# Pooled attention and token/channel mixing on one core: new positions for all attention steps, from a planner that knows later key loads and waits between half banks

## The chip, the cores and the metric

One core of one Trainium2 chip runs the whole program once. The time is device microseconds of one execution, taken as the median of several executions; lower is better. The engines are PE (matmul), ACT, DVE and POOL (elementwise work), and SP, which here only issues DMAs. PE writes its products to PSUM, which ACT and DVE read; POOL works on SBUF alone.

## The reference

```python
# q, k, v: (8, 8, 1152, 64); w_theta, w_ch: (512, 512); w_tok_r, w_tok_i: (576, 576)
q_pool = q.reshape(B, H, S // 2, 2, D).mean(axis=3)
scores = (1 / sqrt(D)) * q_pool @ k.transpose(0, 1, 3, 2)
attn = exp(scores - max(scores)); attn = attn / (sum(attn) + 1e-09)
x = (attn @ v), heads side by side                 # (8, 576, 512)
theta = x @ w_theta
zr, zi = x * cos(theta), x * sin(theta)
u = x + einsum('ts,bsd->btd', w_tok_r, zr) + einsum('ts,bsd->btd', w_tok_i, zi)
out = u + maximum(u @ w_ch, 0)
```

## The kernel before

There are two stages. The first, the attention, goes through 32 pairs of heads; the second goes through 8 batches of x. Weights arrive as 64-bit words and are turned to fp32 in 18 jobs that run beside the attention. The order of the second stage is written out and not touched here.

For a pair of heads the first stage does the following (names of steps as in the planner, lines as in the profile). SP loads q (`load_q`, L609), keys (`load_k`, L635) and v (`load_v`, L668). DVE adds neighbouring q rows (`pool_q`, L652); POOL takes two differences of key blocks (`diff0`, `diff1`, L659), which need all keys of the pair. DVE transposes the keys and q into PSUM (`t1`, L686; `t0`, L684), ACT copies this rounded (`hi10`, `hi0`, L713) and DVE makes the rest (`lo10`, `lo0`, L717). Key loads of the next pair wait for both transposes. PE makes products for the row maxima (`pm`, 15 steps, L730), DVE reduces them (`mx`, 15 steps, L742, then `nm` and `nt`, L750 and L753), and SP lays the negated maxima out (`load_max`, six DMAs, L765). PE makes the scores (`e`, 18 steps, L780), ACT exponentiates each (`x`, L790) into one of 14 buffers, POOL sums them up (`ss`, L797), and PE multiplies them with v (`av`, 18 steps, L802) and sums over keys (`ns`, L823). An exponential's buffer is free again when both `av` and `ss` (or `ns`) have read it. ACT copies the products out (`xu`, L814; `sm`, L834); SP and DVE divide by the sums through DRAM (`norm_...`, L839 to L883) and store x. A step such as x16 is the one of half u = 1 and key tile 6; ss01 and e18 likewise. Some three pairs are in flight at once.

PSUM in this stage is four tiles of two banks. `t`, `pm` and `e` take a tile; an `av` chain and the `ns` chain take one half (`acq=2`).

A weight job fetches (`w_fetch`, L934), splits words on ACT (`w_low`, `w_abs`, L944 and L948) and DVE (L952 to L969), puts them together on POOL (`w_mul`, `w_add`, L974 and L986); weights of the token mixing are then transposed on PE (`w_turn`, L1018 and L1023), the others are split again (L1000, L1005). After the last job its memory is given to x, and `early` issues the first load of x for the second stage (`xload`, L532).

All this is issued in an order that `schedule` finds when the program is built. Each step has an engine, an assumed duration and latency, and what it depends on; the planner runs a clock for the engines, PSUM and the buffers, and emits one step after the other. A step's position is `PLACE[step] + 18 * pair`, a weight step's `w0 + wd * job + wk * offset`. Between the first two pairs and the last, PE, ACT, DVE and POOL take their attention steps strictly in order of position (`ahead` is 1); SP looks 24 steps ahead, and the others 8 at the two ends. The next weight step of an engine is looked at as well, and goes first if its position is lower, or if by the planner's clock it is done before the other step could begin, give or take `slack`:

```python
if best is None or (at < far and (best[0] >= far or at + busy <= best[0] + PLACE["slack"])):
    best = (min(at, far), op, slot, busy)
```

On the chip each engine works its own list in order and waits at semaphores.

Of the kernel before, what the change touches and what calls it, by code (L numbers as in the profile page):

```python
# [25 lines left out]
    "load_k00": -34.88242, "load_k10": -32.47173, "load_k20": -41.45336, "load_k30": -28.50736,  # L26
    "diff00": -39.87507, "diff10": -35.75839, "load_q00": -64.34477, "load_q10": -75.25567,
    "load_q20": -35.82454, "load_q30": -61.16811, "pool_q00": -30.6917, "t10": -29.76226,
    "hi10": -18.79817, "lo10": -28.28938, "t00": -27.58235, "hi00": -17.63187, "lo00": -26.75167,
    "pm40": -19.09444, "mx40": -26.55706, "pm30": -18.78858, "mx30": -25.01085, "pm41": -17.19725,  # L30
    "mx41": -24.62429, "pm31": -17.04758, "mx31": -24.49251, "pm42": -16.56876, "mx42": -22.74469,
    "pm32": -16.06269, "mx32": -20.32787, "pm10": -12.92619, "mx10": -19.29508, "pm00": -15.38721,
    "mx00": -19.72983, "pm11": -11.3469, "mx11": -17.70748, "pm01": -10.92526, "mx01": -17.26176,
    "pm12": -9.29323, "mx12": -17.25916, "pm02": -9.11, "mx02": -16.98715, "pm20": -8.01255,
    "mx20": -16.13332, "pm21": -7.07965, "mx21": -15.98746, "pm22": -6.48707, "mx22": -13.57219,
    "nm00": -12.29583, "nt00": -11.25146, "load_max00": -9.16448, "load_max10": -19.75675,
    "load_max20": -9.6046, "load_max30": -38.55642, "load_max40": -12.38135,
    "load_max50": -76.95718, "e00": 0.83663, "x00": 2.47359, "e02": 1.73308, "x02": 4.44865,
    "e01": 1.85317, "e04": 2.06445, "x01": 5.17463, "x04": 6.56139, "ss01": -1.85432,
    "e03": 3.91959, "x03": 6.7328, "load_v00": -10.05597, "ss02": 1.71669, "e05": 7.91203,  # L40
    "ss03": 2.55261, "x05": 7.83833, "e06": 8.42872, "x06": 8.10801, "e10": 8.86747,
    "e07": 9.67362, "ss04": 3.13891, "x10": 9.26813, "x07": 9.74981, "e11": 10.10462,
    "e08": 10.39007, "x11": 10.98997, "ss05": 5.11849, "x08": 11.4556, "e13": 10.49512,
    "e12": 10.97372, "x13": 12.18436, "ss06": 12.66707, "x12": 14.01721, "e14": 11.21729,
    "e15": 11.32578, "x14": 14.22593, "av00": 12.28953, "x15": 14.10769, "e16": 13.47618,
    "e17": 12.6626, "av01": 12.39451, "ss11": 5.07143, "x16": 16.09668, "av02": 13.93027,
    "x17": 14.34836, "av10": 13.65905, "av03": 13.95031, "ss12": 5.61435, "av11": 13.86236,
    "av04": 14.10402, "av12": 13.94758, "ss13": 7.02357, "av05": 14.82141, "av13": 13.9736,
    "av06": 15.1885, "av14": 14.47683, "ss14": 10.7647, "av07": 18.30814, "av15": 14.8295,
    "av08": 18.38773, "ss15": 12.20219, "av16": 15.17117, "xu00": 20.33264, "e18": 17.01919,  # L50
    "ss16": 12.79139, "x18": 20.2032, "av17": 15.46904, "av18": 19.01658, "xu10": 21.82954,
    "ns00": 23.21575, "ns10": 23.58014, "ns20": 23.98061, "sm00": 25.00175,
    "norm_spread00": 3.09315, "norm_load00": 26.0753, "norm_recip00": 25.31238,
    "norm_save00": 35.09001, "norm_bcast00": 34.4841, "norm_bcast10": -37.21955,
    "norm_out00": 35.37772, "norm_store00": 63.75033, "norm_turn00": 39.55758,
    "norm_store10": -2.85209, "pool_q10": -44.60046, "ns30": -19.16538, "ns40": -12.30378,
# [1344 lines left out]
```

## Time and profile before

| | us |
|---|---|
| median of 3 executions | 1296.65 (1294.09 to 1301.59) |
| profiled execution | 1299.62 |
| its span | 1297.9 |
| attention, to the last run of av products with its end | 0 to about 834 |
| second stage | about 834 to 1297.9 |
| busy in the span: PE, DVE, POOL, ACT | 1229.5, 958.6, 804.6, 665.2 |

The profile is that of one execution. Ends of matmuls are modelled, since they overlap, so a busy PE is not a PE at its peak. "Waits" counts the idle time of an engine in front of an instruction by what ended it.

### The profile page before, as it was taken

What the parts mean: (1) busy time and instruction counts of PE and PEld (TensorE: products, weight loads), DVE (VectorE), ACT (ScalarE), POOL (GpSimd) and SP (SyncE); (2) the same over time, 40 slices, a digit from 0 to 9 for tenths busy, and PEclk for the clock granted to TensorE, in tenths of its full rate; (3) what the DMA queues carried; (4) which work ended last, traced back from release to release, by engine and by line L of the source; (5) the groups of instructions that cost most, each with busy time, mean ns of one, the idle gap of its engine ahead of it and who ended that gap; (6) DMA issues with size and microseconds to landing.
All of it is one profiled execution on the core that took longest, in us unless ns stands there. A gap on an engine that the chain in (4) does not pass through costs nothing.

```text
span 1297.9 us, 27681 instructions
## 1 busy us (share of the span) xinstructions
PE 1229.5 (95%) x10929; PEld 957.3 (74%) x10929; DVE 958.6 (74%) x1311; ACT 665.2 (51%) x1098; POOL 804.6 (62%) x600
## 2 busy tenths in 40 slices
PE   4899999999999998999999999789999999999998
PEld 2566667666666666666666766478999999999997
DVE  6889899989898988899999887265464645637452
ACT  1456556556656655666655665454443443444430
POOL 1678978988987987888889888324423233232320
PEclk9999999999999999999999999989999999999999
DMA  7445564555555447555546642404524425244221
GB/s 119 90 92 126 117 133 118 116 115 146 125 106 138 112 100 157 110 116 122 129 112 140 144 98 89 123 29 103 105 39 93 83 44 107 35 92 90 42 45 37
DMA packets 481201, 130.93 MB, mean 101 GB/s; under 512 B 450976, under 2 KB 451104, under 8 KB 481072
## 3 DMA queue, kind: packets, MB, share of 16 engines
q1 hardware_dynamic: 480896, 128.71, 46.9%
q8 instruction: 86, 1.41, 0.5%
q0 software_dynamic: 176, 0.46, 0.2%
q14 instruction: 43, 0.35, 0.1%
HBM read 97.21 MB, written 30.70 MB: 99 GB/s over the span
## 4 chain that ended last, share of the span: by engine, by line
PE 60%; DVE 10%; POOL 7%; SPq 7%; DMA 6%; ACT 6%; issue 4%; DVEq 0%; POOLq 0%; ACTq 0%
PE py L1221 16%; PE b L802 12%; PE b L780 11%; PE pr L1260 8%; PE pth L1133 7%; PE b L730 5%; POOL ss L797 5%; DVE mx L742 4%; SPq L635 3%; ACT pc L790 2%; PE b L823 2%; DMA dn<-ro 2%; DMA qk<-in_k_dram 2%; ACT hi L713 1%; DVE b L684 1%
## 5 line engine op out<-in xcount | busy, mean ns | idle before, releaser
L797 POOL TENSOR_TENSOR ss<-ss,pc 128x576 f32<-128x576 f32 x314 | 451.9, 1451 | 14.3 <-ACT pc L790 1.9
L742 DVE TENSOR_REDUCE mx<-b 128x2 f32<-128x768 f32 x480 | 433.4, 950 | 30.9 <-PE b L730 26.2
L790 ACT ACTIVATE pc<-b 128x576 f32<-128x576 f32 x576 | 356.2, 650 | 182.0 <-PE b L780 140.1
L802 PE MATMUL b<-pc,vn 128*64 128x288 f32 x2304 | 307.2, 412 | 0.5 <-ACT pc L790 0.5
L802 PEld LDWEIGHTS b<-pc,vn 128*64 128x64 f32 x2304 | 154.1, 136 | 113.4 <-issue 23.4
L1221 PE MATMUL py<-wtk,Z 128*128 128x288 f32 x1728 | 233.7, 296 | 0.0
L1221 PEld LDWEIGHTS py<-wtk,Z 128*128 128x128 f32 x1728 | 232.2, 189 | 1.3
L730 PE MATMUL b<-hi 64*128 64x384 f32 x960 | 186.8, 397 | 30.1 <-DVE mx L742 16.7
L1194 POOL TENSOR_TENSOR Z<-ab,Z 128x512 fp32r<-128x512 f32 x40 | 51.7, 1294 | 258.6 <-ACT Z L1190 258.6
L780 PE MATMUL b<-hi 64*128 64x288 f32 x1152 | 185.2, 318 | 5.1 <-ACT pc L790 2.0
L780 PE MATMUL b<-lo,hi 64*128 64x288 f32 x1152 | 170.6, 292 | 0.0
L780 PE MATMUL b<-hi,lo 64*128 64x288 f32 x1152 | 170.4, 291 | 0.0
L730 PEld LDWEIGHTS b<-hi 64*128 64x128 f32 x960 | 89.6, 188 | 109.1 <-DVE mx L742 57.3
L659 POOL TENSOR_TENSOR qk<-qk 128x384 f32<-128x384 f32 x62 | 63.3, 1021 | 133.3 <-DMA qk<-in_k_dram 72.1
L780 PEld LDWEIGHTS b<-hi 64*128 64x128 f32 x1152 | 108.6, 185 | 38.5 <-ACT pc L790 30.9
L780 PEld LDWEIGHTS b<-lo,hi 64*128 64x128 f32 x1152 | 109.0, 186 | 0.0
L780 PEld LDWEIGHTS b<-hi,lo 64*128 64x128 f32 x1152 | 108.9, 185 | 0.0
L1260 PEld LDWEIGHTS pr<-us,wch 128*128 128x128 f32 x768 | 104.1, 188 | 1.6
L1260 PE MATMUL pr<-us,wch 128*128 128x288 f32 x768 | 105.1, 295 | 0.0
L797 POOL TENSOR_TENSOR ss<-pc,pc 128x576 f32<-128x576 f32 x64 | 101.1, 1580 | 5.2 <-ACT pc L790 5.1
L717 DVE TENSOR_TENSOR lo<-b,hi 128x960 fp32r<-128x960 f32 x64 | 67.4, 1054 | 42.7 <-ACT hi L713 42.7
L713 ACT CAST hi<-b 128x960 fp32r<-128x960 f32 x64 | 56.0, 876 | 79.6 <-DVE b L684 63.1
(95 smaller groups left out, 1324.7 us busy)
## 6 DMA issues: line engine op xcount, KB each, us to landing
vn<-in_v_dram SPq DMA_DIRECT2D x32, 576.0 KB
qn<-in_q_dram SPq DMA_DIRECT2D x124, 144.0 KB
qk<-in_k_dram SPq DMA_DIRECT2D x124, 144.0 KB
dn<-ro SPq DMA_DIRECT2D x64, 144.0 KB
xbd<-xb SPq DMA_DIRECT2D x32, 288.0 KB
xd<-xu SPq DMA_DIRECT2D x32, 288.0 KB
xT<-xd SPq DMA_DIRECT2D x8, 1152.0 KB
xn<-xbd SPq DMA_DIRECT2D x140, 64.0 KB
```

The costliest lines, as they stand in the source:

```text
L659: (nc.vector if op.eng == DVE else nc.gpsimd).tensor_tensor(kn[:, c : c + W], kn[:, c : c + W], kn[:, c - W : c], ALU.subtract)
L713: nc.scalar.copy(hi, src)
L717: nc.vector.tensor_tensor(lo, src, hi.bitcast(F32), ALU.subtract)
L730: nc.tensor.matmul(pm[:, h, 0:W], hi[hs, q : q + P], hi[hs, group(g)], start=(g == 0), stop=True, skip_group_check=(g > 0),)
L742: nc.vector.tensor_reduce(maxima(op.i)[:, at, g : g + 1], slots[op.slot][:, :, 0:W], AX.X, ALU.max)
L780: nc.tensor.matmul(pe[:, h, 0:HALF], w[hs], x[hs], start=bool(op.acq and n == 0), stop=(n == len(terms) - 1), skip_group_check=not op.acq,)
L790: nc.scalar.activation(pc, slots[op.slot][:, :, 0:HALF], AF.Exp, scale=SC)
L797: nc.gpsimd.tensor_tensor(st["ss", u], first, st["pc"][u, k], ALU.add)
L802: nc.tensor.matmul(half(op)[hs, 0:HALF], st["vn"][:, h, key(u, k), :], st["pc"][u, k][:, h, :], start=(k == 0), stop=(k == KT - 1),)
L1133: nc.tensor.matmul(th, xs[c][:, j * P : (j + 1) * P], ws[:, c], start=(n == 0), stop=(n == 11))
L1221: nc.tensor.matmul(st["py", c, u][:, 0:HALF], Z[zi][:, c * P : (c + 1) * P], wtk[wi][:, kw, u * HALF : (u + 1) * HALF], start=(i == 0 and ...
L1260: nc.tensor.matmul(pr[u][:, 0:HALF], wch[wi][:, c, e * P : (e + 1) * P], st["us", ui][:, c, u * HALF : (u + 1) * HALF], start=(n == 0), st ...
```

## The change

All numbers of `PLACE` for the first stage are new, `slack` becomes 0, and the planner that turns them into an order is changed in four ways: q and key loads of all pairs but the first count as landed 2 us later (`LATE`); a step of PE that writes a PSUM tile, or a step that takes one, waits for all reads of that tile, and a step that reads it for all writes, of the other half too; a sum on POOL counts 1.44 us in place of 1.49; and the engines' choices are looked at again after each step that touches PSUM. No step is added or left out, and none changes its engine.

Sorted by position, a period of the steady part runs in this order (only the parts that differ in what the text speaks of; a step stands for the pair that it then belongs to):

```
ACT   before  ... x13 x12 x15 x14 x17 x16 hi10 hi0 x18 xu0 x00 xu1 x02 x01 ...
      after   ... x13 x12 x15 x14 x17 hi10 x16 hi0 x18 xu0 x00 xu1 x02 x01 ...
POOL  before  ... ss15 ss06 ss16 diff0 ss01 diff1 ss02 ss03 ss04 ss11 ss05 ...
      after   ... ss05 ss16 ss06 ss01 diff0 ss02 diff1 ss03 ss04 ss11 ss12 ...
DVE   before  ... mx20 mx21 norm_turn mx22 pool_q nm t1 nt norm_recip lo10 t0 lo0 ...
      after   ... mx20 pool_q mx21 norm_turn mx22 nm nt t1 norm_recip lo10 t0 lo0 ...
PE    before  ... e14 e15 pm22 av00 av01 e17 e16 av10 (12 more av) pm40 e18 pm30 av07 av08 ...
      after   ... e14 e15 av00 pm22 e17 e16 av01 (12 more av) pm30 e18 pm40 av17 av07 av08 ...
```

The diff, of the positions only the lines with those that the text names:

```diff
@@ -23,43 +23,43 @@
 NU = 18
 CHAINS = ((0, 0, 0), (0, 1, 0), (0, 0, 1), (0, 1, 1), (0, 0, 2), (0, 1, 2), (0, 2, 0), (1, 0, 0), (0, 2, 1), (1, 0, 1), (0, 2, 2), (1, 0, 2), (1, 1, 0), (1, 2, 0), (1, 1, 1), (1, 2, 1), (1, 1, 2), (1, 2, 2))
 PLACE = {
-    "load_k00": -34.88242, "load_k10": -32.47173, "load_k20": -41.45336, "load_k30": -28.50736,
-    "diff00": -39.87507, "diff10": -35.75839, "load_q00": -64.34477, "load_q10": -75.25567,
-    "load_q20": -35.82454, "load_q30": -61.16811, "pool_q00": -30.6917, "t10": -29.76226,
-    "hi10": -18.79817, "lo10": -28.28938, "t00": -27.58235, "hi00": -17.63187, "lo00": -26.75167,
...
-    "mx41": -24.62429, "pm31": -17.04758, "mx31": -24.49251, "pm42": -16.56876, "mx42": -22.74469,
...
-    "mx20": -16.13332, "pm21": -7.07965, "mx21": -15.98746, "pm22": -6.48707, "mx22": -13.57219,
-    "nm00": -12.29583, "nt00": -11.25146, "load_max00": -9.16448, "load_max10": -19.75675,
...
-    "load_max50": -76.95718, "e00": 0.83663, "x00": 2.47359, "e02": 1.73308, "x02": 4.44865,
-    "e01": 1.85317, "e04": 2.06445, "x01": 5.17463, "x04": 6.56139, "ss01": -1.85432,
-    "e03": 3.91959, "x03": 6.7328, "load_v00": -10.05597, "ss02": 1.71669, "e05": 7.91203,
...
-    "e15": 11.32578, "x14": 14.22593, "av00": 12.28953, "x15": 14.10769, "e16": 13.47618,
-    "e17": 12.6626, "av01": 12.39451, "ss11": 5.07143, "x16": 16.09668, "av02": 13.93027,
-    "x17": 14.34836, "av10": 13.65905, "av03": 13.95031, "ss12": 5.61435, "av11": 13.86236,
...
-    "av08": 18.38773, "ss15": 12.20219, "av16": 15.17117, "xu00": 20.33264, "e18": 17.01919,
-    "ss16": 12.79139, "x18": 20.2032, "av17": 15.46904, "av18": 19.01658, "xu10": 21.82954,
...
-    "ns50": 43.96992, "slack": 0.16717, "turn": 17.33779, "w0": -5.19739, "wd": 35.76329,
-    "wk": 0.41649, "lk": 1, "early00": 324.36552, "xhi00": 511.24399, "xlo00": 529.88695,
...
+    "load_k00": -34.94071, "load_k10": -32.85543, "load_k20": -30.83893, "load_k30": -35.52884,
+    "diff00": -37.19566, "diff10": -31.28969, "load_q00": -60.55296, "load_q10": -74.72264,
+    "load_q20": -50.02811, "load_q30": -47.22098, "pool_q00": -31.10499, "t10": -29.02451,
+    "hi10": -21.24054, "lo10": -25.1024, "t00": -24.82416, "hi00": -21.04049, "lo00": -24.40739,
...
+    "mx41": -23.44655, "pm31": -15.56925, "mx31": -22.23347, "pm42": -14.09315, "mx42": -21.60018,
...
+    "mx20": -15.4754, "pm21": -7.21938, "mx21": -12.23387, "pm22": -5.43592, "mx22": -11.59812,
+    "nm00": -11.40415, "nt00": -11.03511, "load_max00": -13.97522, "load_max10": -6.62334,
...
+    "e00": 1.41286, "x00": -1.88398, "e02": 4.30492, "x02": -0.66143, "e01": 4.3503,
+    "e04": 4.93721, "x01": 1.87805, "x04": 2.52593, "ss01": -2.51516, "e03": 5.24938,
+    "x03": 3.61403, "load_v00": -30.14112, "ss02": 2.76183, "e05": 6.91915, "ss03": 4.96317,
...
+    "av00": 11.51732, "x15": 13.55609, "e16": 12.667, "e17": 12.59015, "av01": 12.73296,
+    "ss11": 5.40063, "x16": 14.81219, "av02": 14.39006, "x17": 14.0223, "av10": 15.10992,
...
+    "av16": 16.81107, "xu00": 15.63219, "e18": 16.94049, "ss16": 13.45832, "x18": 14.99426,
...
+    "ns40": -25.83351, "ns50": 1.66532, "slack": 0, "turn": 0.91371, "w0": -2.05713,
+    "wd": 36.70137, "wk": 0.6312, "lk": 1, "early00": 308.04233, "xhi00": 428.57106,
...
 LOOK = 8
+LATE = 2.0
 QB = 5
 TURN = (0.1, 0.05, 0.1, 0.04)
 PE, ACT, DVE, POOL, SP = range(5)
@@ -230,7 +230,7 @@
             ran.append((E[u, k], x))
             if 0 < k < tail:
                 first = X[u, 0] if k == 1 else SS[u, k - 1]
-                SS[u, k] = add(POOL, 1.49, 1.43, "ss", i, "ss", g, [x, first] + (back(i, 2, "ns0") if k == 1 else []), a=u, b=k)
+                SS[u, k] = add(POOL, 1.44, 1.43, "ss", i, "ss", g, [x, first] + (back(i, 2, "ns0") if k == 1 else []), a=u, b=k)
                 SS[u, k].reads = [x] + ([X[u, 0]] if k == 1 else [])
         s["ends"] = [E[u, k] for u, k, p in seq if (u, k) not in cont]
         s["ave"], s["xu"], first = [], [], None
@@ -343,7 +343,13 @@
     mode, held, moved = ROW64, 0.0, 0.0
     banks = [0.0] * (2 * SLOTS)
     tokens = [0.0] * PC_BUFS
+    reads, writes = [0.0] * SLOTS, [0.0] * SLOTS
     order = []
+
+    def tile_of(op, slot=None):
+        own = op if op.acq else op.owner
+        n = own.slot if slot is None else slot
+        return n // 2 if own.acq == 2 else n
 
     def pair_slot():
         n = min(range(SLOTS), key=lambda k: max(banks[2 * k], banks[2 * k + 1]))
@@ -372,6 +378,9 @@
                 if op.name not in ("av", "ns") and sum(b < far for b in banks) < (3, 2)[op.acq - 1]:
                     t = far
                 at = far if t >= far else max(at, t + (0.053 if e == PE else 0.04))
+            if at < far and (op.acq or op.owner):
+                n = tile_of(op, slot)
+                at = max(at, reads[n] + 0.053) if e == PE or op.acq else max(at, writes[n])
             if at < far and op.takes:
                 t = min(tokens)
                 at = far if t >= far else max(at, t)
@@ -405,6 +414,8 @@
         if e == SP and op.i != 0:
             t = 0.85 * (op.lat - 1.9)
             op.end = moved = max(op.end - t, moved) + t
+            if op.name in ("load_q", "load_k"):
+                op.end += LATE
         free[e] = at + busy
         if e == PE:
             mode = op.mode
@@ -418,6 +429,13 @@
                 banks[b] = far
         elif op.owner:
             op.slot = op.owner.slot
+        if op.acq or op.owner:
+            n = tile_of(op)
+            if e == PE or op.acq:
+                writes[n] = max(writes[n], op.end + LAG[e][ACT])
+            else:
+                reads[n] = max(reads[n], op.end)
+            todo[PE] = todo[ACT] = todo[DVE] = True
         if op.last:
             own = op.owner
             own.freed = max(own.freed, op.end)
@@ -440,7 +458,7 @@
             if f.wait == 0:
                 todo[f.eng] = True
         if op.acq or op.last:
-            todo[PE] = todo[DVE] = True
+            todo[PE] = todo[DVE] = todo[ACT] = True
         if op.reads:
             todo[ACT] = True
         if e == POOL:
```

## Rows read from the trace of the kernel before

**Rows 1.** Windows, one pair each: start:end, length, busy (instructions) of PE, PEld, DVE, ACT, POOL.

```profile
701.96:725.96 24.00, 23.72 (x249) 16.40 (x247) 23.25 (x29) 14.73 (x25) 19.44 (x15) 1.00 0.54 113
301.18:326.77 25.59, 24.04 (x248) 16.42 (x247) 23.26 (x29) 14.86 (x25) 20.74 (x16) 1.00 0.51 113
501.69:528.43 26.74, 24.04 (x248) 16.42 (x247) 23.20 (x28) 14.65 (x25) 22.08 (x17) 1.00 0.48 101
```

**Rows 2.** Timeline of PE: first and last of the 31 long av runs (start, us).

```profile
55.38 6.53 PE L802 MATMUL b<-pc,vn 128*64 128x288 f32 x52
...
800.13 7.50 PE L802 MATMUL b<-pc,vn 128*64 128x288 f32 x60
```

**Rows 3.** Timeline of PE: four transposes of a token weight.

```profile
798.44 0.66 PE L1018 MATMUL b<-ident,ws 128*128 128x128 f32 x4
```

**Rows 4.** Waits, whole span: who waited for whom, us, times, longest.

```profile
POOL qk L659 <- DMA qk<-in_k_dram: 72.1, 19, 20.0
...
POOL qk L659 <- DVE xu L869: 34.8, 8, 6.9
...
ACT pc L790 <- POOL ss L797: 22.9, 21, 2.9
```

**Rows 5.** Timelines of ACT and DVE, pairs at 301.18 and 501.69; idle before in brackets.

```profile
303.84 0.65 ACT L790 ACTIVATE pc<-b 128x576 f32<-128x576 f32 x1 [1.50 <-POOL ss L797]
...
501.62 1.19 DVE L686 STREAM_TRANSPOSE b<-qk 128x960 f32<-128x960 f32 x1
...
505.76 0.65 ACT L790 ACTIVATE pc<-b 128x576 f32<-128x576 f32 x1 [2.92 <-POOL ss L797]
506.30 0.95 ACT L713 CAST hi<-b 128x960 fp32r<-128x960 f32 x1
...
507.29 1.16 DVE L717 TENSOR_TENSOR lo<-b,hi 128x960 fp32r<-128x960 f32 x1 [2.80 <-ACT hi L713]
508.36 0.98 DVE L684 STREAM_TRANSPOSE b<-qk 128x768 f32<-128x768 f32 x1
```

**Rows 6.** Timeline of POOL ahead of that pair's x16.

```profile
495.00 1.01 POOL L659 TENSOR_TENSOR qk<-qk 128x384 f32<-128x384 f32 x1 [5.00 <-DVE mx L742]
...
497.20 1.43 POOL L797 TENSOR_TENSOR ss<-pc,pc 128x576 f32<-128x576 f32 x1
498.59 1.02 POOL L659 TENSOR_TENSOR qk<-qk 128x384 f32<-128x384 f32 x1
499.56 4.80 POOL L797 TENSOR_TENSOR ss<-ss,pc 128x576 f32<-128x576 f32 x3
```

**Rows 7.** Chain that ended last, between the two stages: start, us, what.

```profile
832.62 0.08 PE b L1023
...
832.82 2.56 DMA xT<-xd
...
848.10 4.10 PE pth L1133 x10
```

**Rows 8.** Groups by line: busy us, mean ns, idle before with what ended it.

```profile
L814 ACT COPY xu<-b 128x288 f32<-128x288 f32 x64 | 25.5, 399 | 36.8 <-PE b L802 35.8 <-PE b L823 1.0
```

**Rows 9.** Timelines of SP, PE, ACT and DVE at the start.

```profile
2.90 2.29 SPq L668 DMA_DIRECT2D vn<-in_v_dram  x1
...
9.30 1.54 PE L698 MATMUL b<-ident,qk 128*128 128x128 f32 x6 [0.30 <-DVE qk L659]
...
11.64 1.28 ACT L944 ACT_TABLE_LOAD   x1 [11.64 <-DMA raw<-in_moe_w_theta_dram]
...
13.49 1.64 ACT L713 CAST hi<-b 128x960 fp32r<-128x960 f32 x2
...
33.86 0.67 DVE L952 TENSOR_SCALAR ws<-wf 128x513 f32<-128x513 f32 x1
```

**Rows 10.** One line's instructions: w_fetch of jobs 2, 6, 10, 14 and 16; first and last start.

```profile
L934 SPq DMA_DIRECT2D raw<-in_moe_w_tok_r_dram x9: 345/462/583, 94.3 to 786.1; - x9
```

**Rows 11.** One line's instructions: pool_q; min/median/max ns, first and last start.

```profile
L652 DVE TENSOR_TENSOR qk<-qn x31: 731/1110/1969, 27.8 to 772.1; 128x576 f32<-128x576 f32 x31
```

37 rows, old and new, of the table PLACE are left out of this document.

## The prediction

> **What bounds the kernel now.** I read the attention by pairs of heads first [rows 1]. The length of one pair differs: 24.00 us at 701.96, 25.59 at 301.18, 26.74 at 501.69. PE's own work in these three is nearly the same (23.72, 24.04, 24.04 us busy), so what makes a pair long is PE waiting, up to 2.7 us of it. Then I took the 13-step run of av products that marks each pair on PE [rows 2]: 31 of them stand between 55.38 and 800.13, so 30 pairs take 744.75 us, 24.83 each, which is 24.75 us more than 30 pairs of 24.00. Of that, the transposes of a token weight, which go through PE between two steps (four take 0.66 us, a fifth follows [rows 3]), explain about 0.75 us in each of the 8 pairs there that carry them: 6 us. The other 18.7 us I looked for in the waits.
>
> The waits of the whole span [rows 4] name it. ACT's exponentials wait 22.9 us, 21 times, for a sum on POOL. Listed by time, 18 of the 21 (21.9 us) are the exponential x16, the last one in front of hi10 on ACT; two of them are shown [rows 5]. The pair at 501.69 has the whole chain. POOL stands still for 5.00 us until the keys of a later pair are there for diff0; then it runs diff0, a weight step, ss01, diff1 and three more sums [rows 6]. x16 cannot start because all 14 exponential buffers are taken, and the one it needs comes free with those sums: it starts at 505.76 after 2.92 us of waiting. hi10, whose input DVE had transposed by 502.8, is behind x16 and starts at 506.30; lo10 on DVE waits 2.80 us for it [rows 5], and all that follows in the pair (t0, hi0, lo0, the maxima) moves with it. The wait of 2.92 us made its pair 2.74 us longer than 24.00; that of 1.50 us at 303.84 made its pair 1.59 us longer [rows 1, 5].
>
> After the last pair there is a second bound. At 832.62 the last weight's last transpose starts; with its end the memory is free into which x is loaded. At 832.82 the load starts, and theta, the first product of the second stage, runs without a stop only from 848.10 [rows 7]. So what the attention gains counts for the kernel only as far as the last weight job comes forward with it.
>
> **The change, part by part.** *ACT: x16 goes behind hi10* (before: x17, x16, hi10, hi0; after: x17, hi10, x16, hi0). Nothing is added. hi10 no longer waits for POOL. What is late next: x16 itself, and hi0 behind it. hi0 needs t0, which ends at 509.34, 2.05 us after lo10 has started on hi10's result [rows 5]; x16 takes 0.65 of these, so 1.4 us of waiting is covered, and of today's 18 waits only that of 2.92 us would show by more than 0.5. On PE x16 is wanted by av16 and e18, late in and after the run of 6.5 us [rows 2]: covered.
>
> *POOL: ss01 goes in front of diff0* (before: ss16, diff0, ss01, diff1, ss02; after: ss06, ss01, diff0, ss02, diff1). POOL waits at its key differences for 72.1 us by the row for keys and for 34.8 by the row that names DVE [rows 4], from the third pair on 28 times. One sum of 1.43 us [rows 6] now fits into that wait, so the sums behind the keys come 1.4 us earlier. By itself that would remove every x16 wait under 1.4 us, 13 of the 18. The wait that it adds: where the keys are in time, diff0 comes up to 1.43 us later, and behind it queue diff1 and, on DVE, t1 of that pair. diff1 ended at 499.6, t1 began at 501.62 [rows 5, 6]: 2.0 us of cover even in this late pair. Nothing; without the cover 1.4 us a pair.
>
> So both edits reach the same 21.9 us. Below, nothing is gained if the sums stay as late as now and hi0 takes the place of hi10. Above, 21.9 us and, since PE was busy in 23.72 of 24.00 us, 0.28 us in each of 30 pairs, 8.4: 30 us. I take 15.5 us, 0.7 of the waits: the 18.7 us found above, which leave the weights' transposes where they are, are the more likely ceiling, and some new waits will come.
>
> *DVE: nt goes in front of t1, pool_q in front of the last two maxima.* t1 takes 1.19 us [rows 5]; the six loads of the maxima may start that much earlier, and the q loads, which wait for pool_q, by the two maxima that it passes. Both thin out the stretch of SP in which q, maxima and key loads follow each other. This helps the keys; I count nothing for it. *PE:* pm22 goes behind the first av step, and av steps change places inside their run; the number of changes between row and column form stays at four av runs and one ns run a pair. Nothing.
>
> *Waits between halves of a bank pair.* The planner now knows that a step on one half also waits for the other. What this costs today is bounded by the one such wait that the trace names: xu, which reads one half, waited 1.0 us in the whole span for ns, which writes the other [rows 8]. Counted as nothing, 1 us at most.
>
> *Start.* The first thing on ACT is w_low of job 0. It waits for the raw weights until 11.64, a table load of 1.28 us and w_low follow, and only then the first hi starts, at 13.49, although PE had begun the last six transposes for it at 9.30 and ended them by 10.84 [rows 9]. In the changed order v of pair 1 (-30.14 + 18 = -12.14) stands in front of w_fetch (-2.06), and neither waits for anything; so the raw weights come later for the planner than the transposes do, and it puts w_low behind both hi. hi then starts between 10.84, if the table load is done by then, and 12.1, if not: gain 2.7 to 1.4 us, on the chain that DVE's first lo and maxima follow. SP needed 2.29 us for the first v; as much later w_low may be, which is covered until w_max at 33.86 [rows 9]. I take 2.0.
>
> *Weights and x.* The due positions of job m move from -5.2 + 35.76 m to -2.06 + 36.7 m, for the last by 19, one pair; and `slack` becomes 0, so that a weight step gets in early only where it fits in whole. Today the jobs step with the pairs: the token fetches of jobs 2 and 16 are 691.8 us apart [rows 10], 49.4 a job, two pairs. And they are early: job 16, due at position 567, is fetched at 786.1, before the run of pair 30 (position 552) has begun at 800.13. So the later positions need not bind. I let the last job keep its place relative to the last pair: nothing.
>
> One rule of the skill speaks against the move of pool_q. pool_q, a sum of two tensors, takes between 0.73 and 1.97 us for the same shape, 1.11 in the median [rows 11], while POOL's sums run. The Trainium skill, page "SBUF — State Buffer", section "Who interferes with whom", says that a DVE instruction with two inputs in SBUF and a GpSimd instruction that reads SBUF shut each other out for a whole instruction; the spread in the trace agrees. By that pool_q would hold up a maximum at its new place; this is rival D below.
>
> **Sum.** 15.5 + 2.0 = 17.5 us. The profiled execution took 1299.6 us (span 1297.9 and 1.7 around it), so 1282.1 after; the three runs have the median 1296.65, 3.0 lower, so **1279**.
>
> **Rivals.**
> *A, more:* pairs go down to PE's own time and all these waits vanish. 30 + 2.7 us: 1264. For it: the keys come earlier too. Against: small waits, 0.1 to 0.3 us, are spread over every pair.
> *B, hidden:* the weights' chain is bound by its own loads and steps and not by the pairs, so the x load stays at 832.8 less the 2 us of the start: 1295. For it: the jobs lie in the gaps of the other work, and gaps are what the change removes. Against: the step of 49.4 us, two pairs.
> *C, slower:* with `slack` 0 a weight step of the last two jobs misses its gap, and the chain ends one pair (24.8 us) later against the attention. Then the x load starts 24.8 - 17.5 = 7.3 us later than now: 1304. It decides from the point where the last transposes come later than 832.6 although the pairs end 17.5 us sooner.
> *D, pool_q:* at its new place every pool_q takes as long as the longest, 1.97 - 1.11 = 0.86 us more in 31 pairs: 26.7 us against 17.5, 1306; with half of it 1292.5. For it: the two maxima behind it feed nm. Against: today it stands between the last maximum and nm, just as much in the way.
>
> **How the numbers follow.** Chances: forecast (1268 to 1289) 0.58, A 0.12, B 0.13, C 0.10, D 0.07, of which 0.05 near 1292 and 0.02 above 1303. A measurement of this kernel tells about 0.5%, 6.5 us, from no change: faster is below 1290.2, slower above 1303.1. Faster: 0.58 + 0.12 = 0.70. Within: B and most of D, 0.18. Slower: C and the rest of D, 0.12. The range from 1262 to 1297 leaves out C, the worst of D and what lies beyond A, some 0.15. The forecast's own range is 1268 to 1289.
>
> **What would show it.** Right: exponentials wait under 6 us for POOL's sums; lo10 waits about 0.9 us for hi10, pair after pair; 30 pairs take some 729 us; the first hi starts before 12.2; the last transposes and the x load come near 815. Wrong: long pairs remain, with x16 or hi0 waiting for POOL (the edits don't reach the sums); or the pairs shrink and the x load stays at 830 or later (B, C); or pool_q's mean rises and the maxima behind it wait (D).

## The result and the profile after

The changed kernel takes 1286.76 us, the median of five executions (1285.66 to 1287.63); the kernel before, in five beside it, 1301.59 (1294.09 to 1304.51). The ratio is 0.9899, its 95% interval 0.9865 to 0.9934: faster by 1.0%; the predicted 1279 us lies 7.8 us lower. The profiled execution took 1287.1 us; its span, from the first to the last instruction, is 1285.3, 12.6 less than before. Lines of the kernel's body stand 18 higher than before (x is L808, the sums L815, `hi` L731, `lo` L735).

I read the same views in the same order. First the pairs, here by windows that each run from one `sm` on ACT to the next (columns as in [rows 1]):

```profile
117.20:141.32 24.12, 23.78 (x248) 16.35 (x250) 21.42 (x27) 14.06 (x24) 22.25 (x17) 1.00 0.63 135
141.32:167.52 26.20, 24.29 (x253) 16.70 (x255) 24.30 (x31) 15.93 (x27) 19.48 (x15) 1.00 0.52 105
...
586.40:612.22 25.82, 24.76 (x253) 16.90 (x255) 23.59 (x31) 16.04 (x28) 19.72 (x15) 1.00 0.50 106
...
660.45:684.57 24.12, 23.77 (x248) 16.33 (x250) 23.20 (x29) 14.46 (x24) 22.51 (x17) 1.00 0.62 133
...
sum 758.88, PE 738.59 PEld 504.96 DVE 673.26 ACT 458.64 POOL 647.15; mean PE 23.83 PEld 16.29 DVE 21.72 ACT 14.79 POOL 20.88
```

The last row sums all 31 windows; for the kernel before the same row is

```profile
sum 764.13, PE 740.79 PEld 507.96 DVE 662.68 ACT 459.43 POOL 636.46; mean PE 23.90 PEld 16.39 DVE 21.38 ACT 14.82 POOL 20.53
```

So the pairs gave 5.25 us, where I had 15.5. The rows with 253 instructions on PE are the windows that carry transposes of a token weight: seven among the first 29. The other 22 fell from 24.73 to 24.27 us on the mean, 10.2 us in all, and 15 of them are now at 24.15 or less (9 before). The seven rose from 25.10 to 25.87, which takes 5.4 us back. The last two windows gave 0.5.

The waits of the whole span (us, times, longest):

```profile
POOL ss L815 <- ACT pc L808: 95.1, 37, 16.6
...
POOL qk L677 <- DMA qk<-in_k_dram: 20.5, 4, 18.5
...
PE b L748 <- DVE mx L760: 14.3, 17, 4.0
...
ACT pc L808 <- POOL ss L815: 10.0, 9, 1.9
```

Against [rows 4]: exponentials wait 10.0 us for POOL's sums in place of 22.9, and POOL's wait for keys is gone but for one at the start (18.5 us). POOL now waits for ACT. DVE's `lo` waits 1.0 us for `hi` at most; before, the longest was 5.2 at the start and 2.80 in the pairs behind it [rows 5]. In the chain of work that ended last PE has 80% (60% before), POOL 1% (7%).

The start on ACT, which answers to [rows 9]:

```profile
0.75 1.28 ACT L731 ACT_TABLE_LOAD   x1 [0.75 <-PEq L1403]
9.17 0.96 ACT L731 CAST hi<-b 128x960 fp32r<-128x960 f32 x1 [7.14 <-PE b L716]
11.01 0.80 ACT L731 CAST hi<-b 128x768 fp32r<-128x768 f32 x1 [0.88 <-PE b L716]
```

```profile
8.26 0.87 PE L716 MATMUL b<-ident,qk 128*128 128x128 f32 x3 [0.39 <-DMA qk<-in_k_dram]
9.43 1.54 PE L716 MATMUL b<-ident,qk 128*128 128x128 f32 x6 [0.30 <-DVE qk L677]
```

The first `hi` starts 4.3 us earlier than at 13.49, the first `sm` 2.9 (67.83, 70.74 before), the last `sm` 8.2 (826.71, 834.87). Theta runs without a stop from 836.47, 11.6 us earlier than in [rows 7]: between the last `sm` and theta another 3.4 us went away. DVE and PE there, first before, then after:

```profile
845.01 0.21 DVE L849 RECIPROCAL rc<-rc 128x9 f32<-128x9 f32 x1 [4.19 <-DMA rc<-rd]
848.10 2.93 PE L1133 MATMUL pth<-wth,xh 128*128 128x512 f32 x6 [7.14 <-DVE xh L543]
```

```profile
833.25 0.89 DVE L561 CAST xh<-xT 128x640 fp32r<-128x640 f32 x2
835.85 0.21 DVE L867 RECIPROCAL rc<-rc 128x9 f32<-128x9 f32 x1 [1.71 <-DMA rc<-rd]
835.98 0.43 DVE L561 CAST xh<-xT 128x640 fp32r<-128x640 f32 x1
```

```profile
836.47 2.93 PE L1151 MATMUL pth<-wth,xh 128*128 128x512 f32 x6 [1.88 <-DVE xh L561]
```

Before, the reciprocal of the last pair stood ahead of the third cast and waited until 845.01 for its load, and two casts with it (PE waited 7.1 us there); now it stands ahead of the fourth alone. The sum of all: 2.9 at the start, 5.25 in the pairs, 3.4 between the stages, and 1.0 in the second stage, 12.6 us. The last of these goes with PE's clock and not with the order of the kernel. In both kernels PE waits some 2.1 us in front of one group of products there; before, the granted clock then stood at 0.5, its 1.2 GHz level, for 3.4 us from 909.5, and in the changed kernel it did not fall:

```profile
908.76 3.21 PE L1133 MATMUL pth<-wth,xh 128*128 128x512 f32 x8 [2.17 <-DVE r L1159]
909.50:912.90 3.40, 3.40 (x9) 2.62 (x9) 2.93 (x7) 1.88 (x4) 0.00 (x0) 0.50 0.00 1
```

```profile
898.21 2.12 PE L1151 MATMUL pth<-wth,xh 128*128 128x512 f32 x8 [2.10 <-DVE r L1177]
```

### The profile page after: what moved, and what is told of

Read it like the earlier page. It is cut to its first block, busy times and chain, and to the rows that moved or that the text cites. A ratio compares the mean times of both kernels' runs of the same rounds, so it can differ in the third digit from the quotient of the medians.

```text
span 1285.3 us, 27898 instructions
## 1 busy us (share of the span) xinstructions
PE 1227.5 (96%) x10929; PEld 955.0 (74%) x10929; DVE 965.0 (75%) x1311; ACT 664.9 (52%) x1098; POOL 814.8 (63%) x600
## 4 chain that ended last, share of the span: by engine, by line
PE 80%; DVE 8%; ACT 7%; issue 3%; DMA 1%; POOL 1%; ACTq 0%; SPq 0%; DVEq 0%; POOLq 0%
PE b L820 22%; PE b L798 17%; PE py L1239 16%; PE pr L1278 8%; PE b L748 7%; PE pth L1151 7%; ACT pc L808 4%; DVE mx L760 4%; PE b L841 4%; ACT Z L1208 1%; DMA qk<-in_k_dram 0%; DVE lo L735 0%; POOL xl L567 0%; DVE xu L887 0%; DVE kk L1175 0%
## 5 line engine op out<-in xcount | busy, mean ns | idle before, releaser
L815 POOL TENSOR_TENSOR ss<-ss,pc 128x576 f32<-128x576 f32 x314 | 460.0, 1478 | 13.6 <-ACT pc L808 1.5
L760 DVE TENSOR_REDUCE mx<-b 128x2 f32<-128x768 f32 x480 | 438.7, 951 | 35.6 <-PE b L748 26.0
L808 ACT ACTIVATE pc<-b 128x576 f32<-128x576 f32 x576 | 355.7, 652 | 182.0 <-PE b L798 127.3
L1212 POOL TENSOR_TENSOR Z<-ab,Z 128x512 fp32r<-128x512 f32 x40 | 51.8, 1294 | 258.4 <-ACT Z L1208 250.8
L748 PE MATMUL b<-hi 64*128 64x384 f32 x960 | 187.2, 390 | 17.3 <-DVE mx L760 14.3
L815 POOL TENSOR_TENSOR ss<-pc,pc 128x576 f32<-128x576 f32 x64 | 104.4, 1631 | 96.6 <-ACT pc L808 93.6
L748 PEld LDWEIGHTS b<-hi 64*128 64x128 f32 x960 | 92.2, 190 | 97.9 <-DVE mx L760 59.0
L798 PEld LDWEIGHTS b<-hi 64*128 64x128 f32 x1152 | 108.7, 185 | 45.7 <-ACT pc L808 35.6
L731 ACT CAST hi<-b 128x960 fp32r<-128x960 f32 x64 | 56.3, 879 | 73.1 <-DVE b L702 42.5
L735 DVE TENSOR_TENSOR lo<-b,hi 128x960 fp32r<-128x960 f32 x64 | 67.6, 1057 | 27.5 <-ACT hi L731 26.4
L1255 DVE TENSOR_TENSOR uT<-xT,py 128x288 f32<-128x288 f32 x64 | 25.4, 448 | 74.8 <-PE py L1239 74.8
```

Of the source, the lines that this page charges most:

```text
L731: nc.scalar.copy(hi, src)
L735: nc.vector.tensor_tensor(lo, src, hi.bitcast(F32), ALU.subtract)
L748: nc.tensor.matmul(pm[:, h, 0:W], hi[hs, q : q + P], hi[hs, group(g)], start=(g == 0), stop=True, skip_group_check=(g > 0),)
L760: nc.vector.tensor_reduce(maxima(op.i)[:, at, g : g + 1], slots[op.slot][:, :, 0:W], AX.X, ALU.max)
L798: nc.tensor.matmul(pe[:, h, 0:HALF], w[hs], x[hs], start=bool(op.acq and n == 0), stop=(n == len(terms) - 1), skip_group_check=not op.acq,)
L808: nc.scalar.activation(pc, slots[op.slot][:, :, 0:HALF], AF.Exp, scale=SC)
```

## The experiments

Executions of the kernel before lay between 1294 and 1309 us, so beside the ratio I read the windows in the trace: first `sm`, the sum of 31 windows, and the mean of the 22 without and the 7 with transposes. Each of these is read from one execution. How far such readings scatter shows where the kernels don't differ: the second stage, from its first product with `xl` to the end, took 445.4 to 447.6 us in the 14 traces (446.2 on the mean in the seven without a stretch at clock 0.5 like that at 909.5, 447.1 in the seven with one; kernels of either order are in both groups), and the stretch from the last `sm` to that product 14.6 to 16.0 us in the seven with the old order there.

| kernel | ratio to before, 95% | span | first sm | 31 windows | 22 | 7 |
|---|---|---|---|---|---|---|
| before | 1 | 1297.9 | 70.74 | 764.13 | 24.73 | 25.10 |
| after | 0.9899 (0.9865 to 0.9934) | 1285.3 | 67.83 | 758.88 | 24.27 | 25.87 |
| e1_start | 0.9962 (0.9941 to 0.9983) | 1293.8 | 68.42 | 764.21 | 24.72 | 25.15 |
| e2_hi_first | 0.9966 (0.9946 to 0.9985) | 1295.2 | 71.03 | 763.05 | 24.68 | 25.00 |
| e3_sum_first | 1.0000 (0.9981 to 1.0018) | 1300.3 | 71.67 | 767.59 | 24.91 | 25.04 |
| f2_moves_hs | 0.9956 (0.9938 to 0.9974) | 1295.1 | 72.44 | 761.43 | 24.58 | 25.16 |
| f1_moves_q | 1.0094 (1.0076 to 1.0111) | 1309.7 | 71.28 | 775.61 | 25.22 | 25.21 |
| f3_moves_all | 1.0120 (1.0101 to 1.0139) | 1314.0 | 72.89 | 780.11 | 25.31 | 25.53 |
| g1_undo_hs | 0.9968 (0.9956 to 0.9980) | 1294.3 | 65.80 | 768.99 | 24.57 | 26.37 |
| g2_undo_q | 1.0093 (1.0075 to 1.0110) | 1310.0 | 67.71 | 782.93 | 24.62 | 28.22 |
| g3_undo_av | 1.0084 (1.0068 to 1.0100) | 1309.2 | 68.09 | 781.43 | 25.07 | 26.57 |
| e4_turn_at_run | 0.9877 (0.9848 to 0.9907) | 1283.9 | 66.70 | 757.91 | 24.26 | 25.75 |
| f4_turn_in_run | 0.9874 (0.9856 to 0.9893) | 1282.1 | 67.56 | 755.58 | 24.28 | 25.34 |
| g4_recip_last | 0.9855 (0.9835 to 0.9875) | 1279.8 | 66.77 | 754.95 | 24.26 | 25.31 |

**The two edits that I had counted on, in the old order.** First each by its position in the plan of before (which lets the planner move other steps too, mostly those of the weights), then both as bare moves in the finished order, from the third pair on (`put` takes a step out of the order and sets it before or behind another; nothing else moves).

```diff
-    "x16": 16.09668     (e2_hi_first)
+    "x16": 17.8
-    "ss01": -1.85432    (e3_sum_first)
+    "ss01": -4.5
```

```diff
+    put("x", 1, 6, 3, "behind", "hi", 1, 0, 2)         # f2_moves_hs
+    put("ss", 0, 1, 3, "before", "diff", 0, 0, 2)
```

> The kernel before with the exponential x16 behind hi10 on ACT and nothing else given. Theory (the prediction's: hi10 waited behind x16 for POOL's sums): the wait of lo for hi falls from 2.8 us at most to about 1 us, the pairs without token transposes fall from 24.73 us on the mean to about 24.3, and the time falls by some 10 us, about 0.8%. Rival (the wait moves on, from hi10 to hi0 or from ACT to av16): pairs stay at 24.7 us and the time within 3 us of before.

> The kernel before with the sum ss01 in front of the key difference diff0 on POOL and nothing else given. Theory (both edits reach the same waits): exponentials wait for POOL's sums 8 us or less in all (22.9 before), the time falls by 5 to 9 us, a little less than with x16 behind hi10. Rival (diff0 comes 1.4 us later in each pair and DVE's transposes of the keys with it): the pairs are as long as before or longer, and DVE waits for POOL's differences in the steady part.

> The kernel before with the two other moves and everything else in its old order: x16 behind hi10 on ACT and ss01 in front of diff0 on POOL, from the third pair on. Theory H: exponentials wait under 6 us for POOL's sums and the pairs without token transposes fall to about 24.3 us, 10 us in all. Theory K: the waits for sums vanish and the pairs stay within 0.1 us of 24.7, because hi10 then waits for t1 and POOL's difference for the keys, as in the run with x16 alone. Theory P: as K.

The waits of the run with x16 alone:

```profile
ACT hi L713 <- DVE b L686: 31.8, 27, 15.1
...
PE b L730 <- DVE mx L742: 23.0, 31, 4.0
...
ACT pc L790 <- POOL ss L797: 3.9, 10, 0.5
```

The same two rows before:

```profile
ACT hi L713 <- DVE b L686: 16.5, 5, 15.1
...
PE b L730 <- DVE mx L742: 16.7, 22, 4.0
```

The wait that I had named is gone, 22.9 us to 3.9, and the pairs are as long as before (24.68 and 24.73). In its place `hi10` waits for t1 itself (31.8 us against 16.5, 15.1 of each once at the start) and PE for maxima (23.0; 16.7). So x16's wait was the last one in front of `hi10`, but t1 was nearly as late. POOL did not hold t1 up: in that run its last key difference had ended 3.5 us or more ahead of every t1, and DVE stood idle in front of t1 for 0.1 us in all 31. t1 came when DVE's own line came to it. Both moves together took 2.7 us off the windows, or some 5, an estimate, if the one of 26.81 us in their trace, where the granted clock stood at 0.5 for 3.4 us, is put at the mean of the others; by the ratio they are worth 5.7 us (3.4 to 8.1), and x16 alone 4.4 (2.0 to 7.0), of which its windows show 1.1. Theory H, 10 us, fails in the old order. For ss01 alone the expected 5 to 9 us fail too: exponentials waited 5.7 us, the windows of its trace grew by 3.5, the time is the same.

**pool_q and nt, which I had counted at nothing,** in the old order, alone and with the other two.

```diff
+    put("pool_q", 0, 0, 3, "before", "mx", 2, 1, -1)   # f1_moves_q; f3_moves_all: with both above
+    put("nt", 0, 0, 3, "before", "t", 1, 0, 1)
```

> The kernel before with two local moves on DVE and everything else in its old order: pool_q in front of the last two maxima and nt in front of t1, from the third pair on. Theory K (the keys): the q loads wait less for pool_q's result, the six loads of the maxima leave earlier, and behind them on SP the keys; so POOL's differences wait less for them and the pairs without token transposes fall from 24.73 us to about 24.4, 8 us in all. Theory H (x16 in front of hi10): the pairs stay at 24.7 us, since x16 and ss01 have not moved. Theory P (neither; the changed kernel's order on PE, with pm22 behind the first av step and other av places, gives the gain): 24.7 us too.

> The kernel before with all four local moves (pool_q, nt, x16, ss01), the orders of PE and SP untouched. Theory K with H: 24.2 to 24.3 us in the pairs without token transposes, 11 us less in all than before. Theory K alone: the same as with pool_q and nt alone, about 24.4. Theory P: 24.7 us.

All three theories fell: 11.5 us more in the windows, not less. Waits on DVE's and SP's work in the run with pool_q and nt:

```profile
POOL qk L670 <- DMA qk<-in_k_dram: 93.0, 19, 20.6
...
PE b L741 <- DVE mx L753: 29.7, 38, 4.0
```

```profile
SPq L894 <- DVE xb L885: 136.4, 32, 5.8
```

The same row before:

```profile
SPq L883 <- DVE xb L874: 99.0, 32, 5.8
```

The keys did not come earlier (93.0 us of waits, 72.1 before), since SP stands in front of the q loads at the store of `norm_turn`'s result (99.0 us before, 136.4 now), and `norm_turn` is behind pool_q on DVE. In the pair at 656.87 pool_q is done at 658.74, the store is issued at 660.32 and the first q load at 661.17; in the changed kernel two of the four q loads stand ahead of that store. And PE waits 13 us more for maxima, since the last two maxima come a pool_q later and `pm22` is still ahead of the first av step.

With all four moves the windows grew by 16.0 us, though x16 and ss01 alone had not made them longer. In that run pool_q itself took longer, 1.64 us in the median (1.11 before, 0.97 in the run with pool_q and nt alone), for the same shape:

```profile
L665 DVE TENSOR_TENSOR qk<-qn x31: 746/1637/2007, 27.9 to 787.4; 128x576 f32<-128x576 f32 x31
```

**The same edits taken out of the changed kernel.**

```diff
+    put("x", 1, 6, 3, "before", "hi", 1, 0, 2)         # g1_undo_hs
+    put("ss", 0, 1, 3, "behind", "diff", 0, 0, 2)
+    put("pool_q", 0, 0, 3, "behind", "mx", 2, 2, -1)   # g2_undo_q
+    put("nt", 0, 0, 3, "behind", "t", 1, 0, 1)
+    put("av", 0, 0, 3, "behind", "pm", 2, 2, 1)        # g3_undo_av
```

> The changed kernel with x16 put back in front of hi10 and ss01 back behind diff0, from the third pair on, all else as it is. Theory S (what shortens the pairs is the keys' earlier landing, which the whole order of SP and DVE gives; the two moves on ACT and POOL matter little once keys are early): pairs without token transposes stay within 0.15 us of 24.27, the time within 3 us of the changed kernel. Theory H (x16 and ss01 give it): exponentials wait some 20 us for POOL's sums again, these pairs go back to about 24.7 us, 10 us in all.

> The changed kernel with pool_q put back behind the last maximum and nt behind t1, from the third pair on; SP keeps its new order, in which the q loads wait for pool_q ahead of nearly everything. Theory S: q loads, loads of maxima and keys all come two to three us later in each pair, POOL waits for keys again (2.0 us of waits from the third pair on now, 20 or more then), and the pairs go to 24.7 us or more, 10 us or more in all. Rival (the keys have more than three us in hand): within 3 us of the changed kernel.

> The changed kernel with the first av step of a pair put back behind the last product of the maxima, pm22, for all but the last two pairs. Theory (pool_q in front of the last two maxima makes DVE free the memory of pm22 later, and the av step is what PE does meanwhile; where only pool_q and nt had moved, PE waited 18.4 us for maxima against 5.9 before): PE waits 10 us or more for maxima (3.4 now) and the time rises by 4 to 12 us. Rival (the seat of one av step is hidden): within 2 us of the changed kernel.

Each costs more than the whole change had gained in the windows: 10.1, 24.1 and 22.6 us. In the run without the new seats of x16 and ss01 the total is the 10 us of theory H, but not by its mechanism: the 22 pairs grew less than H said (24.57), exponentials waited only 9.2 us for sums, and the seven with transposes grew by 0.5. S's bound of 0.15 us failed as well; POOL waits for keys again and PE 8 us more for maxima:

```profile
POOL qk L688 <- DMA qk<-in_k_dram: 69.3, 20, 6.0
...
PE b L759 <- DVE mx L771: 22.3, 33, 4.0
...
ACT pc L819 <- POOL ss L826: 9.2, 6, 1.9
```

Which of the two moves it is in that order was not tried apart.

Without the new places of pool_q and nt, SP waited 134.0 us in front of the q loads (111.1 after), and three windows with transposes took 30 to 33 us. These three hold 16.2 of the 24.1 us. In two of them the edit did more than it should: for two pairs the order now has nt behind two of its own six loads of the maxima, so these loads laid out the maxima of the pair before, and nt, with `lo10` behind it on DVE, waited 3.56 and 4.01 us until they had landed. In the third, ACT's first step of a weight job waited 3.35 us for raw weights whose load stands behind the q loads on SP, and an exponential that PE needed waited behind it.

```profile
562.07 0.21 DVE L782 STREAM_TRANSPOSE nt<-nm 128x32 f32<-128x32 f32 x1 [3.56 <-DMA nmr<-nt]
617.37 0.21 DVE L782 STREAM_TRANSPOSE nt<-nm 128x32 f32<-128x32 f32 x1 [4.01 <-DMA nmr<-nt]
```

```profile
149.03 0.73 ACT L973 ACTIVATE raw<-raw 128x576 f32<-128x576 uint32 x1 [3.35 <-DMA raw<-in_moe_w_tok_i_dram]
```

PE's granted clock (the last column but two of a window's row) then fell to 0.5 as well: from 150.4 for 3.4 us, after PE had waited 3.04 us until 150.3; from 566.8 for 3.4 us, with PE waiting 1.95 us until 564.3 and 1.89 us until 567.0; and from 621.5 for 6.8 us, after 2.95 us of waiting until 620.0.

```profile
621.00:628.50 7.50, 5.80 (x28) 3.27 (x30) 4.75 (x7) 1.96 (x4) 0.00 (x0) 0.54 0.84 118
```

The two windows with the reversed loads are 11.8 us longer than in the changed kernel, so of the 24.1 us some 12 are left for the places of pool_q and nt.

Without the one av step in front of `pm22` 18 of the 22 windows lie between 25.07 and 25.15 us; PE and DVE in one of them:

```profile
686.25 0.44 PE L758 MATMUL b<-hi 64*128 64x384 f32 x2 [0.53 <-DVE mx L770]
```

```profile
684.21 1.12 DVE L680 TENSOR_TENSOR qk<-qn 128x576 f32<-128x576 f32 x1
685.25 0.95 DVE L770 TENSOR_REDUCE mx<-b 128x2 f32<-128x768 f32 x1
```

`pm22` waits for the maximum that pool_q held up; the av step (0.71 us in the changed kernel) was its cover. In all, PE waits 26.3 us for maxima, 14.3 in the changed kernel: 12.0 of the 22.6 us; the rest was not taken apart. This step I had put down as "Nothing".

**The start alone.**

```diff
+    "p1:load_v00": -12.14112
```

> The kernel before with one due position more: v of pair 1 goes ahead of the first fetch of raw weights on SP, so that both first hi stand in front of w_low on ACT; the rest of the order stays. Theory (the changed kernel gets its early start from this and not from the keys): the ACT table load stands at about 0.8 instead of 11.64, the first hi starts at about 9.2 instead of 13.49, the first ns group ends about 3 us sooner, the 30 pairs keep their 744.75 us, and the time falls by 2 to 4 us, too little to tell from the runs but seen in the trace. Rival (the gain is hidden by w_max or by the keys of the next pairs): the first hi starts early and the long av run of pair 1 still stands at 79 to 80.

As the theory has it: the table load stands at 0.75, `hi` at 9.08, the first `sm` 2.3 us earlier, the windows 764.21. The load of x was 2.2 us earlier, and theta ran without a stop from 844.98, 3.1 us earlier. The other 1.0 of its 4.1 us of span lies in the second stage, where this trace has no stretch at the lower clock and that of before has one.

**The pairs with transposes.** In the changed kernel, pair at 586.40, on PE, ACT and DVE:

```profile
594.99 0.63 PE L1036 MATMUL b<-ident,ws 128*128 128x128 f32 x4
...
603.61 0.44 PE L748 MATMUL b<-hi 64*128 64x384 f32 x2 [0.67 <-DVE lo L735]
```

```profile
595.76 0.86 ACT L1055 CAST wtk<-b 128x512 fp32r<-128x512 f32 x2 [1.54 <-PE b L1041]
596.64 0.65 ACT L808 ACTIVATE pc<-b 128x576 f32<-128x576 f32 x1
...
598.55 0.96 ACT L731 CAST hi<-b 128x960 fp32r<-128x960 f32 x1
```

```profile
595.09 0.21 DVE L771 STREAM_TRANSPOSE nt<-nm 128x32 f32<-128x32 f32 x1
596.65 0.69 DVE L1059 TENSOR_TENSOR wtk<-b,wtk 128x512 fp32r<-128x512 f32 x1 [1.34 <-ACT wtk L1055]
597.32 1.19 DVE L704 STREAM_TRANSPOSE b<-qk 128x960 f32<-128x960 f32 x1
```

ACT stands 1.54 us at the casts of the weight until the transposes are through, with x17 behind it (596.64, done at 597.29). DVE stands 1.34 us for the casts, with t1 behind it (597.32). `hi10`, `lo10` and a product of PE follow late. I tried another seat of the transposes alone, then x17 ahead of the casts (which puts t1 ahead of the subtraction too) with the transposes a little later again, behind the first av step:

```diff
+            if op.name == "w_turn" and op.pos < 560:
+                op.pos += (10.53 - op.pos + 9.0) % 18 - 9.0    # e4_turn_at_run
+                op.pos += (12.9 - op.pos + 9.0) % 18 - 9.0     # f4_turn_in_run
+            if op.name == "w_thi" and op.pos < 560:
+                op.pos += (14.03 - op.pos + 9.0) % 18 - 9.0    # f4_turn_in_run
```

> The changed kernel with one more line in the planner: the due position of each token weight's transposes is moved to the nearest place between the last e step and the long av run, so that they no longer stand in the middle of the e and pm steps. Theory (the transposes' new seat is what ate up the gain: they take a memory tile that the next e or pm step needs, and hold it until DVE has read it): the seven pairs with transposes fall from 25.87 us on the mean to about 25.1, the level of the kernel before, 5 us in all, and the time is some 5 us, 0.4%, below that of the changed kernel. Rival (these pairs are long because of the work on the weights on DVE and ACT that they carry, wherever the transposes stand): they stay at 25.9 us and the time does not move against the changed kernel.

> The changed kernel with two more lines in the planner: the transposes of a token weight are due behind the first av step of the long run, and ACT's casts of them behind x17. Theory (in the changed kernel x17 stands behind these casts, which wait for the transposes; t1 wants the memory tile that x17 frees, and behind t1 come hi10, lo10 and the next products of PE, which waited 0.67 us for lo): x17 starts as soon as its product is there, t1 no longer waits for it, the seven pairs with transposes fall from 25.9 to about 25.1 us (24.11 and the 0.98 us of PE that the transposes take), 5 us in all. Rival (DVE's and ACT's own work on the weights makes these pairs long): they stay above 25.6 us.

The first seat alone did little (25.75): my first theory, that the transposes keep a tile from the next e step, explains 0.12 us a pair. With x17 ahead of the casts the seven fell to 25.34, 3.7 us in all; what of this the second seat gives by itself was not tried. The 25.1 us of the theory were not reached:

```profile
592.09 0.65 ACT L812 ACTIVATE pc<-b 128x576 f32<-128x576 f32 x1 [1.46 <-PE b L824]
592.71 0.86 ACT L1059 CAST wtk<-b 128x512 fp32r<-128x512 f32 x2
```

```profile
592.77 1.20 DVE L708 STREAM_TRANSPOSE b<-qk 128x960 f32<-128x960 f32 x1 [1.07 <-DMA qn<-in_q_dram]
```

t1 starts 0.03 us after x17's end in both kernels (597.29 and 597.32; 592.74 and 592.77), which speaks for the tile that x17 frees, although the last row names a load of q. The planner's own list of tiles bears this out for the last run: there t1 takes the tile of x17 in the seven pairs with transposes and in no other, it waits in these (0.73 to 1.34 us), and it starts 0.03 to 0.04 us after x17's end each time. In the changed kernel t1 takes x17's tile in two of the seven, this pair among them; in the other five it takes a tile that a maximum frees, and DVE's line is what is left.

**Between the stages,** on top of that: the last pair's reciprocal behind all four casts of x.

```diff
+    op = [o for o in order if o.name == "norm_recip"][-1]
+    order.remove(op)
+    order.insert(max(order.index(o) for o in order if o.name == "xhi") + 1, op)
```

> The changed kernel with the transposes due in the av run (as in the run before) and one more move: the last pair's reciprocal, which waits on DVE for a load and holds back the last cast of x, goes behind the four casts. Theory (between the two stages PE waits for the casts of x, and these wait on DVE behind the reciprocal): the theta products run on without the wait of 1.9 us, and the time is 1 to 2 us below that with the transposes moved alone. Rival (the norm chain of the last pair, which the reciprocal starts, is needed just as much): no gain, theta's end waits for the last store of x.

```profile
828.14 1.29 DVE L569 CAST xh<-xT 128x640 fp32r<-128x640 f32 x3
829.91 0.22 DVE L875 RECIPROCAL rc<-rc 128x9 f32<-128x9 f32 x1 [0.48 <-DMA rc<-rd]
```

```profile
828.68 3.73 PE L1159 MATMUL pth<-wth,xh 128*128 128x512 f32 x7 [0.47 <-DVE xh L569]
832.21 1.91 PE L1159 MATMUL pth<-wth,xl 128*128 128x512 f32 x4
```

The wait of 1.8 us that PE had there is gone. The next products (xl) start 12.15 us after the load of x was issued, 14.34 without the move: 2.2 us. The span is 2.3 us shorter, but this sum hides two differences of 1.4 and 1.3 us that the move does not explain: the last `sm` comes 1.4 us earlier, and the second stage takes 1.3 longer, with a stretch at the lower clock that the run before has not. With a median of 1281.15 us this version beats both kernels: 1.45% below before by the ratio, and its span is 5.5 us below that of the changed kernel (they did not run side by side; the ratios to before, 0.9855 and 0.9899, have intervals that overlap a little).

## Why the prediction was right, and where its sum was wrong

The side, the range and the forecast's own range (1268 to 1289) held; the steps less well, and part of the hit is luck. The largest term gave a third of its 15.5 us, and 3.4 us came from a place that had no term. The base was off too: the forecast counted down from a median of 1296.65 us of three executions, and the five of the result have 1301.59, so by the medians 14.8 us were gained where 17.5 were forecast.

*x16 and ss01, 15.5 us.* The step that failed is the term of 15.5 us itself, that what makes a pair long is the wait of x16, and that 0.7 of these waits is gained. The waits went as foretold in direction (10.0 us left, "under 6" was missed; none of the nine is in front of a `hi`), but of the 5.25 us the windows gave, they are no separate share: alone in the old order both moves are worth 2.7 us in the windows and 5.7 by the ratio, taken out of the new one 10.1. A row of waits names the last thing that was late, and t1 stood close behind x16.

*pool_q, nt and the order on PE, "Nothing".* Wrong by the largest sums: some 12 us (24.1 with the two windows of reversed loads) and 22.6 us when undone, and 11.5 us of loss when pool_q and nt move alone. The moves hang together: pool_q early needs the av step in front of `pm22` not to hurt, which the undone step shows, and the q loads ahead of the store on SP to be of use, which is read from the rows of SP; no run moved SP's loads by themselves. Rival D had the place right (the maxima behind pool_q wait, where the av step does not cover them) and for the changed kernel the reason wrong: pool_q's median is 1.145 us after, 1.110 in [rows 11], so it is not longer, it is only in front. In the old order with all four moves D's reason was there as well (1.64 us).

*Transposes, left where they are.* They were not: 0.75 us a pair was their work on PE by the prediction's estimate, and their pairs grew by 0.77 more in the new order, 5.4 us in all. With the x17 run, 3.7 of these came back, which shows that much of it to be what queued behind them.

*Start, 2.0 us (1.4 to 2.7).* Measured 2.9 at the first `sm`, 4.3 at the first `hi`. The bound of 2.7 let `hi` start at 10.84, with the end of the last six transposes. That was a misreading: these six belong to the second `hi`, which starts at 11.01; the first has nine others, which ended at 9.13, and it starts at 9.17. The lower bound of 1.4 let the table load wait for data too; it stood at 0.75, ahead of the `hi` that waits, where it had stood at 11.64 behind the wait for raw weights. The Trainium skill, page "ScalarE: Activation LUTs", section "What ACT_TABLE_LOAD costs", gives about 1283 ns, and both traces agree (1.28 us).

*Weights and x.* The last job kept its place at the last pair as assumed: its last transposes start 2.3 us ahead of the last `sm` (824.39 and 826.71), 2.7 before. B and C did not come about. That they came at 824.4 and not near 815 is the missing gain in the pairs.

*Between the stages, not priced.* 3.4 us in these two traces. From the last `sm` to the first product with `xl` it is 12.2 to 12.8 us in the six traces with the new order there, 14.6 to 16.0 in the seven with the old one, and 10.5 in g4_recip_last, which shows that the rest of that wait was of the same kind. Two things changed, the reciprocal's place and how soon its load landed (last section); they were not tried apart. The Trainium skill, page "PSUM — Partial Sum Buffer", section "Engine vs sequencer instructions", says that the queues of ACT, DVE and POOL are strictly first in, first out. The trace agrees: the cast behind the reciprocal, whose input had landed with that of the casts before, stood there for the 1.71 us that the reciprocal waited. *Half banks:* `xu` waited 1.9 us for `ns`, 1.0 before: nothing, as said. What the planner's new counts do by themselves, and the new order of SP, apart from the whole order that came out, was not tried.

## What to carry to other kernels

Before a wait is booked as a gain, look how late the next producer behind the same consumer is, and book only the difference. Moves in a software pipeline whose engines work in order are not a sum: pool_q and nt, which cost 0.9% when they moved alone, cost about as much again when taken out of the new order, so test both ways, and see that an edited order still has each step behind what it needs. An instruction that waits for another engine or a load delays everything behind it in its queue, so put it behind whatever is ready; here that gave up to 3.7 us in the pairs with transposes and 2.2 between the stages.

## What was not expected of the hardware

The reciprocal's input (`rc`) landed and was used 5.87 us after its issue before (839.14 to 845.01), where a part of the load of x had been issued 2.1 us ahead of it, and 3.78 us after in the changed kernel (832.07 to 835.85), where that was 4.3 us ahead: the wait between the stages shrank by this too. The other traces agree: 4.56 to 5.87 us in the seven with the old order there, where that part was issued 1.9 to 2.1 us ahead, and 3.18 to 4.23 in the seven with the new one, where it was 3.2 to 4.3 ahead. In the kernel before, two more loads of x were issued just before that part (835.99), so what delays the small load stays open.
